# Packed attention and a gated feed-forward layer on one core: batch 1's transposes, v1's permute and v2's load in another order

## The chip, the cores and the metric

One core of a Trainium2 chip runs the whole program. Its engines work at the same time, each through its own queue in order: TensorE (PE, matmuls and transposes; PEld is its weight load), VectorE (DVE), ScalarE (ACT), GpSimd (POOL) and SyncE (SP, which only issues transfers). The metric is the device time of one execution in microseconds (us); lower is better.

## The reference, cut to what matters

For 8 batches of 8 heads, 576 positions and a head dimension of 64, 32 packed queries `p` first attend to keys and values, and then every query attends to the 32 packed results. The output of all heads goes through a feed-forward layer with the activation h cos(h).

```python
def sm_attn(qq, kk, vv):
    s = scale * np.matmul(qq, kk.transpose(0, 1, 3, 2))
    a = np.exp(s - np.max(s, axis=-1, keepdims=True))
    a = a / (np.sum(a, axis=-1, keepdims=True) + 1e-09)
    return np.matmul(a, vv)
p_packed = sm_attn(p, k, v)
out = sm_attn(q, p_packed, p_packed)
x = out.transpose(0, 2, 1, 3).reshape(4608, 512)
h = x @ w_in                      # 512 x 2048
return (h * np.cos(h)) @ w_out    # 2048 x 512
```

## The kernel before

The kernel works batch by batch, with an order written out by hand: what the Python code says first is queued first on each engine.

**One batch.** k, q and v come in as 96 partitions x 8 heads x 384 elements, cast to bf16 by a transfer that POOL issues (`load`, L83). k and q are needed transposed: by PE through PSUM in three groups of eight transposes (`pe_T`, L94 to L106; the matmuls are L103, the copies out of PSUM L74 on ACT or L76 on DVE), or by a transposing transfer on SP (`xbar`, L92). Batches 0 and 1 take `pe_T`, the later ones `xbar`. `permute_v` (L85) copies v into an order by position, on POOL or DVE. `pack_p` (L111) transposes the packed queries of some batches (matmul L116) and copies them into `P2` (DVE, L118); it needs `p_bf`, which POOL casts from `p_raw` (`dup_p`, L327). `s1` computes the packed scores (L128) and their exponentials `a1` (ACT, L137). `a1_pe` transposes `a1` in two halves (L161, copies to `a1T` on DVE), and later batches do it by a transfer (`a1_xbar`, L151). `pp` multiplies `a1T` with the permuted v (L169) and puts the packed result into `ppT` (L175, L179). `s2` makes the second scores (L128 again) and exponentials `a2u` (L210), `sums2` and `normalise` the weights `a2n` (L218 to L228). `ppw` multiplies the packed result with `w_in` in four column blocks (L193, into `PPW`). Then 16 steps `h_mm` follow, one for each block of 128 hidden units: four matmuls (L241), the cosine on ACT (L245), the product on DVE (L248, into `gT`). After steps 7 and 15 POOL copies a rest into `joint` (L252).

**The filler.** The product with `w_out` of a batch is spread over the work of the next one. `out_gen` (L286) yields after each matmul (L294), and `fill(n)` issues n of them. For batch 0 there are 64, and the first 32 take two chunks of output rows in turn, four hidden blocks at a time:

```python
    for f0 in range(0, NFC, 4):
        for c in grp:
            for fc in range(f0, f0 + 4):
```

Hidden block fc reads row block fc of `w_out_bf`, which comes in four loads of four blocks each (`load_w_out`, L322). Steps 12 to 15 of batch 0 issue two fillers each.

**Queues and buffers.** POOL issues all loads in this order: k0, v0, q0, `w_in` in four parts, the rest of p, k1, `w_out` parts 0 and 1, v1, q1, `w_out` parts 2 and 3, k2; then, once v1 has been permuted and batch 0's rests copied, q2, k3, and behind a one-element copy called `gate` (L433), which waits for the transposed k3, v2 and q3. q and v have one input buffer each, k has two. SP issues the transposing transfers and the stores of the output (L301), in order. PSUM has three two-bank buffers `psA` and two one-bank buffers `ot`; the latter hold the filler's sums, and in batch 0's steps the results of `ppw`, `pack_p` and `pe_T` for k1. Four `osb` buffers take the output before it is stored.

**Between the steps of batch 0 and those of batch 1** the order is: s1(1), 4 fillers, q1 transposed, the loads of q2 and k3, 2 fillers, half of a1, 2 fillers, the other half, 3 fillers, pp(1), 5 fillers, s2(1), the first block of ppw(1), the transposes of k2, q2 and k3 on SP, the gate and the loads behind it, 4 fillers, the second block of ppw(1), the weights, 11 fillers, and then `slot(1, ...)` with batch 1's 16 steps.

Of the kernel before, what the change touches and what calls it, by code (L numbers as in the profile page):

```python
# [9 lines left out]
BF16 = mybir.dt.bfloat16  # L10
# [5 lines left out]
def kernel(  # L16
# [37 lines left out]
    V, ACT, G = nc.vector, nc.scalar, nc.gpsimd  # L54
# [17 lines left out]
    def copy(eng, out, in_):  # L72
        if eng is ACT:
            ACT.copy(out=out, in_=in_)  # L74
        else:
            eng.tensor_copy(out=out, in_=in_)  # L76

    def psa(dt=FP32):
        return A.tile([128, 2, 512 if dt == FP32 else 1024], dt, name="psA", tag="A")

    def load(n, b):
        bf[n, b] = bf_pool.tile([TP, H, C * D], BF16, name=n + "bf", tag=n + "bf", bufs=2 if n == "k" else 1)
        G.dma_start(out=bf[n, b], in_=srcs[n][b].rearrange("h (p c) d -> p h (c d)", c=C))  # L83

    def permute_v(b, eng=G):  # L85
        vp[b] = vp_pool.tile([TP, C, H * D], BF16, name="vp", tag="vp")
        copy(eng, vp[b].rearrange("p c (h d) -> p c h d", h=H),
             bf["v", b].rearrange("p h (c d) -> p c h d", c=C))
# [5 lines left out]
    def pe_T(n, b, engs=(V, V, V), groups=(0, 1, 2), own=False):  # L94
        if 0 in groups:
            xT[n, b] = att_pool.tile([128, H * 3, TP], BF16, name=n + "T", tag=n + "T", bufs=2 if n == "k" else 1)
        t = xT[n, b]
        flat = bf[n, b].rearrange("p h x -> p (h x)")
        for i in groups:
            ps = bank(BF16) if own else psa(BF16)[:, 0, :]  # L100
            for j in range(8):
                o = 8 * i + j
                nc.tensor.transpose(ps[:, j * TP:(j + 1) * TP], flat[:, o * 128:(o + 1) * 128],  # L103
                                    ident[0:TP, 0:TP])
            copy(engs[i], t[:, 8 * i:8 * i + 8].rearrange("p a x -> p (a x)"),
                 ps[:, 0:8 * TP])  # L106

    def bank(dt=FP32):
        return O.tile([128, 512 if dt == FP32 else 1024], dt, name="ot", tag="ot")

    def pack_p(b0, b1, flat=None):  # L111
        ng = 2 * (b1 - b0)
        if flat is None:
            flat = psa(BF16).rearrange("p a x -> p (a x)")
        for g in range(ng):
            nc.tensor.transpose(flat[:, g * 128:(g + 1) * 128],  # L116
                                p_bf[:, 2 * b0 + g].rearrange("p t d -> p (t d)"), ident)
        V.tensor_copy(out=P2[:, b0:b1].rearrange("p b h n -> p (b h n)"), in_=flat[:, 0:ng * 128])  # L118
# [14 lines left out]
    def s1(b):  # L133
        ps = scores(P2[:, b], xT["k", b])
        sm = small.tile([128, 2], FP32, name="sums1")
        for y in range(2):
            ACT.activation(  # L137
                out=a1[b % 2][:, y, :, 0:TP].rearrange("p (e m) x -> p e m x", e=2),
                in_=ps[y][:, :, 0:HS].rearrange("p e (m x) -> p e m x", m=3),
                func=AF.Exp, scale=scale, accum_out=sm[:, y:y + 1])  # L140
        sums1[b] = sm
# [12 lines left out]
    def a1_pe(b, ys=(0, 1)):  # L154
        if 0 in ys:
            a1T[b] = att_pool.tile([128, 2, C, 128], BF16, name="a1T", tag="a1T")
        t = a1T[b]
        for y in ys:
            ps = psa(BF16)
            for c in range(C):  # L160
                nc.tensor.transpose(ps[0:TP, 0, c * 128:(c + 1) * 128], a1[b % 2][:, y, c, 0:TP], ident)  # L161
            copy(V, t[0:TP, y].rearrange("p c x -> p (c x)"), ps[0:TP, 0, 0:C * 128])

    def pp(b):
        ps = psa()
        for hp in range(4):
            for j in range(C):
                c = 2 * (j % 3) + j // 3
                nc.tensor.matmul(ps[:, 0, hp * 64:(hp + 1) * 64], vp[b][:, c, hp * 128:(hp + 1) * 128],  # L169
                                 a1T[b][0:TP, :, j, 32 * hp:32 * hp + 32], start=(j == 0), stop=(j == C - 1))  # L170
        pv = ps[:, 0, 0:256].rearrange("p (a y x) -> p a y x", a=4, y=2)
        t = ppT[b % 2].rearrange("p (a y) x -> p a y x", y=2)
        for y in range(2):
            r = slice(64 * y, 64 * y + 64)
            V.tensor_copy(out=t[r, :, y, :], in_=pv[r, :, y, :])  # L175
        for y in range(2):
            r = slice(64 * y, 64 * y + 64)
            z = slice(64 - 64 * y, 128 - 64 * y)
            ACT.copy(out=t[z, :, y, :], in_=pv[r, :, y, :])  # L179

    def ppw(b, n, eng=None, own=False, later=False):
        if b not in PPW:
            PPW[b] = ppw_pool.tile([128, 2, DF], BF16, name="PPW", tag="PPW")
        two = isinstance(eng, tuple)
        if own:
            ps = [bank(), bank()]
        else:
            t = psa()
            ps = [t[:, 0, :], t[:, 1, :]]
        for x in range(4):  # L190
            for y in range(2):
                r = slice(64 * y, 64 * y + 64)
                nc.tensor.matmul(ps[y][32 * x:32 * x + 32, :], ppT[b % 2][r, 2 * x + y, :],  # L193
                                 w_in_bf[r, x, n * 512:(n + 1) * 512], start=True, stop=True)

        def evacuate():
            if own or two:
                for y in range(2):
                    copy(eng[y] if two else eng, PPW[b][:, y, n * 512:(n + 1) * 512], ps[y])
            else:  # L200
                copy(eng or (V, ACT)[n % 2], PPW[b][:, :, n * 512:(n + 1) * 512], t)
        if later:
            return evacuate
        evacuate()

    def s2(b):
        a2u[b] = att_pool.tile([128, 2, S], BF16, name="a2u", tag="a2u")
        ps = scores(ppT[b % 2], xT["q", b])
        for y in range(2):
            ACT.activation(out=a2u[b][:, y].rearrange("p (e x) -> p e x", e=2),  # L210
                           in_=ps[y][:, :, 0:HS], func=AF.Exp, scale=rs1[b][:, y:y + 1])
# [21 lines left out]
    def h_mm(b, fc):  # L233
        if fc == 0:
            gT[b] = g_pool.tile([128, NFC, S], BF16, name="gT", tag="gT")
            if b % 2 == 0:
                joint[b // 2] = j_pool.tile([128, NFC, 128], BF16, name="joint", tag="joint")
        ps = psa()
        for y in range(2):
            for e in range(2):  # L240
                nc.tensor.matmul(ps[:, e, 0:HS], PPW[b][:, y, fc * 128:(fc + 1) * 128],  # L241
                                 a2n[b][:, y, e * HS:(e + 1) * HS], start=(y == 0), stop=(y == 1))
        cs = cos_pool.tile([128, S], BF16, name="cosT")
        csv = cs.rearrange("p (e x) -> p e x", e=2)
        ACT.activation(out=csv, in_=ps[:, :, 0:HS], func=AF.Sin, bias=PI_HALF)  # L245

        def rest():
            V.tensor_tensor(out=gT[b][:, fc, :].rearrange("p (e x) -> p e x", e=2),  # L248
                            in0=ps[:, :, 0:HS], in1=csv, op=ALU.mult)
            if fc % 8 == 7:  # L250
                j0 = (b % 2) * 64
                G.tensor_copy(out=joint[b // 2][:, fc - 7:fc + 1, j0:j0 + 64],  # L252
                              in_=gT[b][:, fc - 7:fc + 1, 512:576])
        return rest
# [56 lines left out]
    def fill(n):  # L311
        while n > 0 and filler[1] > 0:
            next(filler[0])
            filler[1] -= 1
            n -= 1
# [53 lines left out]
    load_w_out(3)  # L369
    dup_p(2, 16, G)  # L370
    load("k", 2)
    permute_v(1, G)
    s2(0)
    ppw(0, 0)
    sums2(0, 0)
# [6 lines left out]
    for fc in range(NFC):  # L382
        h_mm(0, fc)()
        if fc in (3, 6):
            ppw(0, 2 + fc // 6, (ACT, V), own=True)
        if fc == 7:
            pack_p(1, 3, bank(BF16))
        if fc in (9, 10, 11):
            pe_T("k", 1, (V, ACT, V), (fc - 9,), own=True)
        if fc >= 12:  # L390
            fill(2)

# [20 lines left out]

    ACT.preload_act_table_set(EXP_SET)
    s1(1)
    fill(4)
    pe_T("q", 1)
    load("q", 2)
    load("k", 3)
    fill(2)  # L420
    a1_pe(1, (0,))
    fill(2)
    a1_pe(1, (1,))
    recips(1)
    fill(3)
    pp(1)
    fill(5)
    s2(1)
    ppw(1, 0, V)
    xbar("k", 2)  # L430
    xbar("q", 2)
    xbar("k", 3)
    G.tensor_copy(out=gate, in_=xT["k", 3][0:1, 0, 0:1])  # L433
    load("v", 2)
    load("q", 3)
    fill(4)
    ppw(1, 1, V)
# [103 lines left out]
```

## Time and profile before

| | us |
|---|---|
| median of 5 runs | 258.52 |
| the five runs | 258.33, 258.33, 258.52, 259.96, 260.72 |
| the profiled execution, its time | 259.96 |
| its span, first to last instruction | 258.2 |
| PE busy in the span | 239.7 (93%) |
| DVE / ACT / POOL busy | 163.3 / 166.4 / 58.8 |
| 512 matmuls of w_out (L294) | 135.5 |
| 512 matmuls of h (L241) | 83.3 |
| mean granted clock of TensorE | 0.987 |
| moved by DMA | 37.67 MB, 146 GB/s |

The span lies 1.8 us under the time of the same execution. A busy PE is not PE at its peak: matmuls are pipelined, and their ends are modelled, so shares of PE add up to more than the work.

PE is by far the busiest engine over the span, but the share is an average. The front, where the inputs and all weights have to come in, differs from the rest: from 4 to 52 us the DMA engines are busy throughout, at about 205 GB/s.

In the rows below, a line of a timeline gives start, duration, engine, source line, operation, what is written and read, the number of instructions merged, and in brackets how long the engine stood idle before and what ended that.

### The profile page before, as it was taken

The page shows a single profiled execution, that of the slowest core. Times are in us where ns is not written, and L with a number is a line of the kernel's source. Part 1 is how long each engine was busy: PE and PEld are TensorE (multiplying, and loading weights), DVE is VectorE, ACT ScalarE, POOL GpSimd, SP SyncE. Part 2 cuts the span into 40 slices and gives each one's busy share as a digit, 9 for nine tenths or more (in the row PEclk, how much of TensorE's full clock was granted, in tenths as well). Part 3 has the DMA queues.
Part 4 walks back from the last instruction along what each step waited for, and adds up shares of the span by engine and source line. Part 5 has one row for each costly group of instructions (what it writes and reads, how often), then busy time and mean ns, then how long its engine had stood idle before and what let it go on. Part 6 is the DMA issues. An engine that isn't in the chain of part 4 may idle for free.

```text
span 258.2 us, 5022 instructions
## 1 busy us (share of the span) xinstructions
PE 239.7 (93%) x2013; PEld 133.1 (52%) x2013; DVE 163.3 (63%) x252; ACT 166.4 (64%) x272; POOL 58.8 (23%) x70
## 2 busy tenths in 40 slices
PE   8777687989999999999999999999999999999993
PEld 3444445546544555455545654565446554565453
DVE  2549873579837777577856775579656764786110
ACT  1368681397769767886887757777786675874000
POOL 8523316000372222504050405020410000000000
PEclk9999996899999999999999999999999999999999
DMA  6999999998989969999989993989291111111232
GB/s 90 203 207 225 205 204 206 203 175 184 158 139 187 217 137 179 224 206 163 221 117 221 154 203 93 166 172 185 69 188 43 41 43 41 41 43 56 66 81 81
DMA packets 65254, 37.67 MB, mean 146 GB/s; under 512 B 37856, under 2 KB 60640, under 8 KB 65232
## 3 DMA queue, kind: packets, MB, share of 16 engines
q0 software_dynamic: 23168, 18.81, 47.8%
q1 hardware_dynamic: 41904, 18.42, 34.3%
q8 instruction: 15, 0.25, 0.4%
q10 hardware_dynamic: 160, 0.13, 0.2%
q14 instruction: 7, 0.06, 0.1%
HBM read 37.22 MB, written 9.44 MB: 181 GB/s over the span
## 4 chain that ended last, share of the span: by engine, by line
PE 70%; DMA 13%; ACT 8%; DVE 4%; issue 2%; POOL 1%; DVEq 0%; ACTq 0%; POOLq 0%
PE ot L294 41%; PE psA L241 18%; DMA qbf<-in_q_dram 12%; DVE gT L248 3%; PE psA L193 3%; ACT cosT L245 2%; ACT a2u L210 2%; DMA a1T<-a 2%; PE psA L169 1%; PE psA L218 1%; PE psA L128 1%; PE ot L280 1%; PE psA L103 1%; ACT L481 1%; PE psA L161 1%
## 5 line engine op out<-in xcount | busy, mean ns | idle before, releaser
L294 PE MATMUL ot<-w_out_bf,gT 128*128 128x512 bf16 x512 | 135.5, 383 | 0.0
L248 DVE TENSOR_TENSOR gT<-psA,cosT 128x576 bf16<-128x576 f32 x128 | 93.0, 754 | 30.0 <-ACT cosT L245 28.7
L245 ACT ACTIVATE cosT<-psA 128x576 bf16<-128x576 f32 x128 | 81.8, 652 | 26.7 <-PE psA L241 25.0
L241 PE MATMUL psA<-a2n,PPW 128*128 128x288 bf16 x512 | 83.3, 286 | 3.2 <-DVE gT L248 1.9
L294 PEld LDWEIGHTS <-gT 128*128 128x128 bf16 x512 | 48.0, 98 | 42.4 <-issue 6.5
L241 PEld LDWEIGHTS <-PPW 128*128 128x128 bf16 x512 | 49.7, 98 | 36.8 <-issue 7.5
L76 DVE CAST PPW<-psA 128x1024 bf16<-128x1024 f32 (+1 forms) x24 | 27.0, 1132 | 11.4 <-PE psA L193 11.4
L252 POOL COPY joint<-gT 128x512 bf16<-128x512 bf16 x16 | 9.8, 616 | 79.0 <-DVE gT L248 79.0
L76 POOL COPY vp<-vbf 96x3072 bf16<-96x3072 bf16 x7 | 19.7, 2809 | 17.9 <-DMA vbf<-in_v_dram 17.9
L76 DVE COPY osb<-ot 128x512 f32<-128x512 f32 (+1 forms) x19 | 12.8, 672 | 16.9 <-PE ot L294 13.8
L74 ACT COPY osb<-ot 128x512 f32<-128x512 f32 (+1 forms) x18 | 10.3, 573 | 18.5 <-PE ot L294 13.8
L228 DVE SCALAR_TENSOR_TENSOR a2n<-a2u,r,lns 128x576 bf16<-128x576 bf16 x16 | 12.4, 815 | 11.5 <-ACT lns L226 11.5
L179 ACT CAST ppT<-psA 64x128 bf16<-64x128 f32 x16 | 4.2, 260 | 19.2 <-DVE ppT L175 16.2
L220 ACT ACTIVATE lns<-psA 128x576 f32<-128x576 f32 x16 | 10.3, 652 | 5.8 <-PE psA L218 5.3
L137 ACT ACTIVATE a<-psA 128x576 bf16<-128x576 f32 x16 | 10.3, 649 | 4.2 <-PE psA L128 4.1
L294 PE MATMUL ot<-w_out_bf,joint 128*128 128x512 bf16 x48 | 12.8, 379 | 0.0
L210 ACT ACTIVATE a2u<-psA,rs 128x576 bf16<-128x576 f32 x16 | 11.0, 737 | 1.3 <-PE psA L128 1.0
L193 PE MATMUL psA<-w_in_bf,ppT 64*32 64x512 bf16 x232 | 10.8, 381 | 0.9 <-DVE gT L248 0.5
L245 ACT ACT_TABLE_LOAD x8 | 10.3, 1283 | 0.1
L226 ACT ACTIVATE lns<-lns 128x576 f32<-128x576 f32 x16 | 10.0, 678 | 0.0
L332 PE MATMUL ot<-wz 128*128 128x512 bf16 x25 | 8.4, 489 | 1.2 <-DVE wz L344 1.2
L74 ACT CAST PPW<-psA 128x1024 bf16<-128x1024 f32 (+1 forms) x9 | 7.3, 821 | 3.2 <-PE psA L193 3.2
(65 smaller groups left out, 144.8 us busy)
## 6 DMA issues: line engine op xcount, KB each, us to landing
kbf<-in_k_dram POOLq DMA_DIRECT2D x8, 576.0 KB, 11.8
vbf<-in_v_dram POOLq DMA_DIRECT2D x8, 576.0 KB, 6.5
qbf<-in_q_dram POOLq DMA_DIRECT2D x8, 576.0 KB, 8.8
out_dram<-osb SPq DMA_DIRECT2D x24, 192.0 KB, 2.4
out_dram<-osb SPq DMA_DIRECT2D x22, 128.0 KB, 2.4
w_in_bf<-in_moe_w_in_dram POOLq DMA_DIRECT2D x4, 512.0 KB, 14.9
w_out_bf<-in_moe_w_out_dram POOLq DMA_DIRECT2D x4, 512.0 KB, 20.9
out_dram<-osb SPq DMA_DIRECT2D x26, 64.0 KB, 2.0
```

The source lines that it names most:

```text
L74: ACT.copy(out=out, in_=in_)
L76: eng.tensor_copy(out=out, in_=in_)
L137: ACT.activation(out=a1[b % 2][:, y, :, 0:TP].rearrange("p (e m) x -> p e m x", e=2), in_=ps[y][:, :, 0:HS].rearrange("p e (m x) -> p e m ...
L193: nc.tensor.matmul(ps[y][32 * x:32 * x + 32, :], ppT[b % 2][r, 2 * x + y, :], w_in_bf[r, x, n * 512:(n + 1) * 512], start=True, stop=True)
L210: ACT.activation(out=a2u[b][:, y].rearrange("p (e x) -> p e x", e=2), in_=ps[y][:, :, 0:HS], func=AF.Exp, scale=rs1[b][:, y:y + 1])
L220: ACT.activation(out=lns[b][:, y].rearrange("p (e x) -> p e x", e=2), in_=ps[:, :, 0:HS], func=AF.Ln)
L226: ACT.activation(out=lns[b][:, y], in_=lns[b][:, y], func=AF.Exp, scale=-1.0)
L228: V.scalar_tensor_tensor(out=a2n[b][:, y], in0=a2u[b][:, y], scalar=r1[b][:, y:y + 1], in1=lns[b][:, y], op0=ALU.mult, op1=ALU.mult)
L241: nc.tensor.matmul(ps[:, e, 0:HS], PPW[b][:, y, fc * 128:(fc + 1) * 128], a2n[b][:, y, e * HS:(e + 1) * HS], start=(y == 0), stop=(y == 1))
L245: ACT.activation(out=csv, in_=ps[:, :, 0:HS], func=AF.Sin, bias=PI_HALF)
L248: V.tensor_tensor(out=gT[b][:, fc, :].rearrange("p (e x) -> p e x", e=2), in0=ps[:, :, 0:HS], in1=csv, op=ALU.mult)
L294: nc.tensor.matmul(pss[c], w, w_out_bf[:, fc, :], start=(fc == 0), stop=(fc == NFC - 1))
```

## The change

The packed-key transposes of batches 1 and 2 go from step 7 of batch 0 to step 12, behind k1's transposes. v1 is permuted by DVE right after s1(1), not by POOL. q1 is transposed behind pp(1), no longer behind the first four fillers, and with it go the loads of q2 and k3 that stand behind it. The numbers of fillers between are 8, 2, 3 and 4 where they were 4, 2, 2, 3 and 5. v2's load stands directly behind k3's, no longer behind the gate. The order of POOL's loads among each other stays as it was.

```diff
--- before.py
+++ after.py
@@ -369,7 +369,6 @@
     load_w_out(3)
     dup_p(2, 16, G)
     load("k", 2)
-    permute_v(1, G)
     s2(0)
     ppw(0, 0)
     sums2(0, 0)
@@ -383,10 +382,10 @@
         h_mm(0, fc)()
         if fc in (3, 6):
             ppw(0, 2 + fc // 6, (ACT, V), own=True)
-        if fc == 7:
-            pack_p(1, 3, bank(BF16))
         if fc in (9, 10, 11):
             pe_T("k", 1, (V, ACT, V), (fc - 9,), own=True)
+        if fc == 12:
+            pack_p(1, 3, bank(BF16))
         if fc >= 12:
             fill(2)
 
@@ -413,25 +412,25 @@
 
     ACT.preload_act_table_set(EXP_SET)
     s1(1)
-    fill(4)
-    pe_T("q", 1)
-    load("q", 2)
-    load("k", 3)
-    fill(2)
+    permute_v(1, V)
+    fill(8)
     a1_pe(1, (0,))
     fill(2)
     a1_pe(1, (1,))
     recips(1)
     fill(3)
     pp(1)
-    fill(5)
+    pe_T("q", 1)
+    load("q", 2)
+    load("k", 3)
+    load("v", 2)
+    fill(4)
     s2(1)
     ppw(1, 0, V)
     xbar("k", 2)
     xbar("q", 2)
     xbar("k", 3)
     G.tensor_copy(out=gate, in_=xT["k", 3][0:1, 0, 0:1])
-    load("v", 2)
     load("q", 3)
     fill(4)
     ppw(1, 1, V)
```

## The prediction

> **What bounds the kernel now.** I read the page's slices first, then the chain of waits from 36 to 56 us, then PE's timeline and a table of windows over the same stretch, and last the landing of single DMA issues.
>
> ```profile
> PEclk9999996899999999999999999999999999999999
> DMA  6999999998989969999989993989291111111232
> ```
>
> Of 40 slices of 6.45 us the granted clock falls in two alone, from 38.7 to 51.6 us, while the DMA engines are full. From slice 8 on PE is busy nine tenths and the chain is nearly all PE: a microsecond lost at the front stays lost. The change lies in and around these two slices. The chain there:
>
> ```profile
> 19.65 20.72 DMA qbf<-in_q_dram
> 40.37 0.05 issue
> 40.41 1.46 PE psA L103 x16
> ...
> 47.75 1.08 PE ot L294 x5
> 48.83 0.57 PE psA L128 x16
> ```
>
> q1's load, issued at 19.65, lands at 40.37; all that follows hangs on it, up to the second scores (s2(1), L128) at 48.8. PE's timeline:
>
> ```profile
> 36.48 0.56 PE L128 MATMUL psA<-kT,P 64*32 64x288 bf16 x16
> 36.98 1.04 PE L294 MATMUL ot<-w_out_bf,gT 128*128 128x512 bf16 x4
> 40.41 2.27 PE L103 MATMUL psA<-ident,qbf 96*128 96x96 bf16 x24 [2.40 <-DMA qbf<-in_q_dram]
> 42.48 1.05 PE L294 MATMUL ot<-w_out_bf,gT 128*128 128x512 bf16 x2
> ```
>
> After s1(1) and four filler matmuls PE stands 2.40 us for q1. Then everything takes twice its time: two fillers 1.05 us, where four took 1.04. The windows (PE, PEld, DVE, ACT, POOL busy; clock; DMA share; GB/s) give the same:
>
> ```profile
> 38.02:40.41 2.39, 0.00 (x0) 0.00 (x0) 0.00 (x0) 1.46 (x5) 2.39 (x2) 0.96 1.26 207
> 40.41:47.04 6.63, 6.62 (x49) 4.63 (x50) 3.02 (x7) 0.00 (x0) 2.54 (x4) 0.50 1.27 203
> 47.04:48.76 1.72, 1.72 (x29) 0.94 (x26) 0.58 (x2) 0.26 (x1) 0.00 (x0) 1.00 1.31 204
> ```
>
> The stall costs 2.4 us and half of 6.63 at clock 0.50, 3.3 more: 5.7 us in all. Transfers move 203 to 207 GB/s here, so landing times are set by the order of issue on the POOL queue. The load of third w_out rows, issued at 21.91:
>
> ```profile
> w_out_bf<-in_moe_w_out_dram POOLq DMA_DIRECT2D x1, 512.0 KB, 21.0
> ```
>
> It lands at 42.9. The fourth, issued 24.59 and 20.9 us under way, lands at 45.5; v1 at 37.5 (16.60 + 20.9); k1 at 29.4 (8.36 + 21.1); k2 at 48.4 (28.71 + 19.7). The change moves no load that stands ahead of these in the queue, so I take all of these times over.
>
> **Packed-key transposes behind k1's.** Before, PE waits 1.89 us in step 7 (until 28.82) for POOL's p_bf. After, steps 8 and 9 (1.14 us as at 29.05) follow at 26.93 and end near 28.1, and the next wait is k1's landing: 1.3 us instead. From the first k1 transposes (30.03) to s1(1) (36.48) went 6.45 us; the four moved transposes add 0.23 (28.82 to 29.05), and a wait of 0.48 for VectorE's copy of kT may go. So s1(1) at 29.45 + 6.45 + 0.23 = 36.1, or 35.7. VectorE copies P2 0.42 us as before. Gain 0.3 to 0.8, but only up to the next fixed landing.
>
> **v1 on VectorE.** POOL loses 2.75 us, for which only its two joint copies waited. VectorE gets 0.96 (batch 0's row at 10.57), after v1 lands at 37.5. Queued behind it are the a1T copies, whose transposes cannot start before ScalarE's first exponential: it ran 38.12 to 38.77. VectorE idles 3.67 us here now. Cost nothing; if v1 came 1 us later, it would delay those copies, and pp(1), by about that.
>
> **q1 behind pp(1).** Eight fillers in a row, 8 x 0.26 = 2.1 (from four in 1.04), run from 36.6 to 38.1 or a bit more, then a1_pe's first half (0.54) until about 38.5. Then fill(2). Fillers are yielded one matmul at a time: eight in steps 12 to 15 and these eight use up w_out rows 0 to 7 of both chunks. The 17th reads row block 8, of the third load: PE stands until 42.95. In the kernel before, the 17th came at 45.5 and found it landed. So the wait is not removed but changes its owner: 42.95 instead of 40.41, 4.4 us instead of 2.40, with less work left behind it.
>
> That work, at half clock by the chain's rows from 40.41 to 48.76: two fillers 0.85, six a transposes 0.64, three fillers 1.28, pp 1.2 (estimate: 24 took 0.80 in a stretch of which most had full clock), 24 q transposes 2.07, four fillers 1.7: 7.7 us, s2(1) at 50.7. At full clock: 0.43 + 0.54 + 0.65 + 0.80 + 1.2 + 0.87 = 4.5, and about 0.5 because the third q group needs the PSUM buffer of pp, which VectorE and ScalarE empty in 0.61 + 0.55: 47.9. How much of it has half clock? 2.40 us of idling cost 6.8 us of it before; 4.4 us I take to cost as much, but its start is open: from 40.2 on as before, it would hold until 47.0 and s2(1) comes near 49.2; from 43.6, until 50.4. I take 50.0, the upper middle, because the slow time seen before began when the stall was nearly over: 1.2 later than 48.76. Bounds: -0.9 and +2.0.
>
> A rule speaks against this edit. The Trainium skill, "TensorE: Matmul & The Clock Gate", section "Why this matters for your kernels", asks for no idle gaps over about 3 us, since the clock then halves; its window (3.4 us) is said to run freely. Here 2.40 us was enough, so the measurement goes below the rule. By the rule alone only the new gap would halve the clock, by the row both do; the sum would be the same.
>
> 17 fillers instead of 16 stand ahead of s2(1): one less later, -0.22 (217 ns each at full clock).
>
> **q2, k3 and v2 loads.** On POOL q2 waits for the last q1 transpose. That was 42.68, and becomes about 48.5, so the queue runs dry after k2 (48.4). A load alone takes 6.4 us (v2 at 65.32); q2 lands near 55 (51.25 before), k3 near 58 (54.75), v2 near 61. On SP the transposes of q2 and k3 wait for these; k3's landed 10.0 us after its load (64.76), so 68 now. Needed: kT3 by s1(3) at 75.2, qT2 by s2(2) at 77.7, each about a microsecond later now. Seven us of cover; beyond it each us is a PE stall. SP's stores queue behind k3's transposes: four o buffers hold all of batch 0's chunks, and the next is filled after 70. v2 ahead of the gate: its permute is no longer tied to a landing at 71.75, but to the gate (68), q3's issue (0.77) and a joint copy (0.62): done near 72.3 instead of 74.55, while pp(2) stood at 75.58 and shows no wait for it. Worth 0 here. v3 and k4 go 2 us earlier; from this, or from PE's own delay, pp(4)'s wait of 0.59 us for a1T can vanish: 0 to -0.6, taken -0.3.
>
> **Sum.** The profiled execution took 259.96 us (span 258.2): + 1.2 - 0.2 - 0.3 gives 260.7, 0.8% over the median of 258.52. Three of the five runs lie at 258.33 to 258.52; whether they, too, had the half clock, no row tells. With the stall but full clock s2(1) would stand 3.3 earlier; pp(2) would then wait about 2.3 for v2 (its cover is 1.0), so 1.0 would be left: 259.0. That is near those runs, a sign that the half clock does not fall on each of them.
>
> **Rivals.**
> - *The replaced wait costs little* (0.24): the same theft by w_out, but with half clock seldom or short, or the shift of +0.7 applied to 258.5. For it: the tight group of runs and s2(1) at 47.9 (259.96 - 0.9 - 0.2 - 0.3 = 258.6). 258.5 to 259.9.
> - *The slow clock outlasts the stage* (0.15), clearly slower: half clock until about 54, as the long gap spans two periods. fill(11) then takes 5.4 us for 2.54, of which the chain from s2(1) to the first h matmul (48.76 to 53.98, nearly all PE) hides next to nothing: s2(1) at 50.7 (+2.0) and another 0.3 to 2.0. It decides once the clock is still 0.5 at 51 us. 261.6 to 263.5.
> - *The stall really goes* (0.06), the other side: if third w_out rows land before they are wanted, 5.7 us vanish up to s2(1), v2 is early enough not to take it back, and 254 to 255.5 results. Against: the landing at 42.9, behind q1 in the same queue.
> - That v2's early load slows the gate by its own transfer (about 3 us, the spacing of loads in the full queue) is inside the seven us above.
>
> **Numbers.** My forecast (259.9 to 261.6, likeliest 260.7) has 0.55. From no change a measurement can tell about 1%: 255.9 to 261.1. About two thirds of the forecast lies below 261.1 (0.36), with the first rival 0.60 for within 1%; slower 0.19 + 0.15 = 0.34; faster 0.06. The range 258.5 to 262.2 leaves out the last rival, and the outer parts of the other two.
>
> **What would show it.** PE waiting in L294 for w_out_bf until 42.9, right after the first six L161 transposes, with no wait of L103 for q; k1's transposes waiting for kbf until 29.4 and L116 for nothing; the granted clock at 0.5 somewhere between 41 and 51; s2(1) near 50; q2's issue near 48.5; pp(2) and pp(4) without waits. I am wrong if the 17th filler does not wait, if the clock stays full, or if PE stands for kT or qT near 70 to 78.

## The result and the profile after

| | before | after |
|---|---|---|
| median (runs) | 259.19 us (48) | 260.67 us (27) |
| lowest and highest | 257.54, 263.8 | 259.01, 264.33 |
| profiled execution: time, span | 259.96, 258.2 | 259.26, 257.1 |
| its mean granted clock | 0.987 | 0.999 |

The ratio is 1.0054, with a 95% interval from 1.0033 to 1.0076: about 1.4 us slower, under the 1% that a measurement of this kernel was taken to tell. The median of before moved from the 258.52 of five runs to 259.19 with 48.

The two profiles shown do not compare like with like: the changed kernel's has the shorter span, although its median is the longer. Its profiled execution is also one of its fastest (259.26, with 259.01 the lowest), and that of the kernel before one of the slower half. The slices of the page after (first the granted clock, then the DMA engines) show what else differs:

```profile
PEclk9999999999999999999999999999999999999999
DMA  6999999699999979999989994989291111112232
```

Counted from 0, slices 6 and 7 had the lower clock before; in this execution they have full clock. In the DMA row slice 7 (45 to 51 us) falls from 9 to 6: from 45.35 on only k2 is left of the loads, until q2 is issued at 47.39. The chain of waits after, over the same stretch (start, duration, what):

```profile
22.02 20.78 DMA w_out_bf<-in_moe_w_out_dram
42.80 0.04 issue
42.84 0.59 PE ot L294 x2
...
47.95 0.37 PE psA L128 x16
```

Where q1's load stood there now stands the third part of w_out, landing at 42.80. PE's timeline after (start, duration, line, operation, count, and in brackets the idle time before it and what ended it):

```profile
37.13 0.56 PE L128 MATMUL psA<-kT,P 64*32 64x288 bf16 x16
37.63 1.90 PE L294 MATMUL ot<-w_out_bf,gT 128*128 128x512 bf16 x8
39.56 0.54 PE L161 MATMUL psA<-ident,a 128*96 128x128 bf16 x6
42.84 0.59 PE L294 MATMUL ot<-w_out_bf,gT 128*128 128x512 bf16 x2 [2.74 <-DMA w_out_bf<-in_moe_w_out_dram]
...
47.88 0.44 PE L128 MATMUL psA<-qT,ppT 64*32 64x288 bf16 x16
```

The wait for q1 before L103 is gone. After eight fillers and six transposes the next filler stands 2.74 us. From there PE works at full clock, and s2(1) starts at 47.88, 5.1 us behind the landing; before, it was 8.4 us behind q1's. Two windows of the profile after (PE, PEld, DVE, ACT, POOL busy; clock; DMA share; GB/s):

```profile
40.10:42.84 2.74, 0.00 (x1) 0.00 (x0) 0.55 (x1) 0.04 (x1) 0.00 (x0) 1.00 1.25 207
42.84:47.88 5.04, 4.40 (x63) 2.90 (x62) 2.95 (x8) 0.52 (x2) 0.49 (x1) 1.00 0.89 140
```

A fair comparison needs the kernel before with full clock at this place, or the changed kernel with the half clock; the experiments gave both.

### The profile page after: what moved, and what is told of

Its sections match the earlier page's. It is cut to its first block, busy times and chain, and to the rows that moved or that the text cites. A ratio compares the mean times of both kernels' runs of the same rounds, so it can differ in the third digit from the quotient of the medians.

```text
span 257.1 us, 5020 instructions
## 1 busy us (share of the span) xinstructions
PE 236.4 (92%) x2013; PEld 130.8 (51%) x2013; DVE 164.6 (64%) x253; ACT 166.6 (65%) x272; POOL 56.4 (22%) x69
## 4 chain that ended last, share of the span: by engine, by line
PE 65%; DMA 14%; ACT 8%; DVE 7%; issue 2%; POOL 2%; DVEq 0%; ACTq 0%; POOLq 0%
PE ot L294 40%; PE psA L241 17%; DMA w_out_bf<-in_moe_w_out_dram 8%; DMA w_in_bf<-in_moe_w_in_dram 6%; DVE gT L248 6%; ACT cosT L245 3%; PE psA L193 3%; PE ot L280 1%; PE psA L218 1%; PE psA L169 1%; PE psA L128 1%; ACT a2u L210 1%; ACT L480 1%; DVE osb L76 1%; ACT osb L74 1%
## 5 line engine op out<-in xcount | busy, mean ns | idle before, releaser
L294 PE MATMUL ot<-w_out_bf,gT 128*128 128x512 bf16 x512 | 133.7, 379 | 3.3 <-DMA w_out_bf<-in_moe_w_out_dram 2.7
L294 PEld LDWEIGHTS <-gT 128*128 128x128 bf16 x512 | 47.9, 98 | 46.2 <-issue 9.9
L252 POOL COPY joint<-gT 128x512 bf16<-128x512 bf16 x16 | 10.5, 657 | 87.2 <-DVE gT L248 87.2
L74 ACT COPY osb<-ot 128x512 f32<-128x512 f32 (+1 forms) x18 | 10.3, 573 | 18.5 <-PE ot L294 13.8
L76 POOL COPY vp<-vbf 96x3072 bf16<-96x3072 bf16 x6 | 16.5, 2751 | 6.9 <-DMA vbf<-in_v_dram 6.9
L332 PE MATMUL ot<-wz 128*128 128x512 bf16 x25 | 7.5, 450 | 1.2 <-DVE wz L344 1.2
```

What stands on the lines that cost most here:

```text
L294: nc.tensor.matmul(pss[c], w, w_out_bf[:, fc, :], start=(fc == 0), stop=(fc == NFC - 1))
```

## The experiments

All ratios are to the kernel before on the same chip.

**The kernel before, again.** No edit.

> The kernel before once more, to see its granted clock run by run beside its time. Clock theory (the runs' spread is the half clock falling on some of them): runs at a clock near 1.00 lie together, those near 0.987 (6.8 us of half clock) 1.5 to 3.3 us above them. Rival (the half clock is absorbed later, the spread has another source): time does not follow the clock. Both: ratio 1.00.

Measured: ratio 0.9997 (0.996 to 1.0035), median 259.49; mean clock per run between 0.983 and 0.993, time from 257.56 to 262.84. No run had a clock above 0.993, so the clock theory's comparison could not be made as it was put. The profiled execution is the fastest of the twelve (span 255.8 us) at the lowest mean clock, 0.983: the mean clock over the whole execution does not order the times, and to that extent the rival holds. PE's timeline of this execution shows that the place of the half clock differs:

```profile
28.73 0.61 PE L116 MATMUL ot<-ident,p_bf 128*128 128x128 bf16 x4 [1.46 <-POOL p_bf L327]
...
39.97 0.85 PE L103 MATMUL psA<-ident,qbf 96*128 96x96 bf16 x16 [0.87 <-DMA qbf<-in_q_dram]
...
45.68 0.64 PE L128 MATMUL psA<-qT,ppT 64*32 64x288 bf16 x16
...
73.27 0.87 PE L169 MATMUL psA<-a1T,vp 96*128 96x64 bf16 x24 [0.71 <-DVE rs L147]
```

The half clock fell earlier (15.1 to 18.5 and 28.7 to 32.2 us); PE comes to q1 later and waits only 0.87 us, and q1's stretch has full clock. So s2(1) is at 45.68, 3.1 us ahead of the first profile. Further on pp(2) stands 0.71 us: the row names DVE, but POOL's permute of v2 ends at 73.21, just before it:

```profile
70.47 2.74 POOL L76 COPY vp<-vbf 96x3072 bf16<-96x3072 bf16 x1 [5.10 <-DMA vbf<-in_v_dram]
```

Set beside the changed kernel at full clock:

| us | s2(1) | s1(2) | pp(2) | s2(2) | span |
|---|---|---|---|---|---|
| before, again | 45.68 | 67.23 | 73.27 | 75.37 | 255.8 |
| after | 47.88 | 69.30 | 74.57 | 76.67 | 257.1 |
| difference | 2.20 | 2.07 | 1.30 | 1.30 | 1.3 |

These are two single executions, but their spans differ by about as much as the medians (1.5 us). The change costs 2.2 us up to s2(1); 0.8 of that come back at pp(2), where the kernel before waits for v2; 1.3 us reach the end, which is 0.5%, as measured. Not all of the 2.2 is the wait: about 0.35 us is that the loads landed earlier in the one execution (q1 at 39.92 against 40.27), and 0.22 that the changed kernel has one filler more ahead of s2(1).

**Matmuls in the gaps.** Their results are not used; the rest of the computation is whole.

```diff
 (before)                      (after)
     fill(4)                       a1_pe(1, (0,))
+    warm_a(10)               +    warm_a(11)
     pe_T("q", 1)                  fill(2)
```

> The kernel before, with ten idle-time matmuls of 512 columns (about 2.2 us) in the 2.40 us in which PE waits for q1; their result is not used. Clock theory: the half clock behind the stall is gone, the mean clock is 0.995 or more in every run, and where the kernel before had it the time falls by 1 to 2 us, so 0.2 to 0.6% in the median. Rival (the stall itself is the cost, the clock is not): ratio 1.00, within 0.2%.

> The changed kernel, with eleven idle-time matmuls (about 2.4 us) behind the first half of the a transposes, in the 2.74 us in which PE waits for the third part of w_out; their result is not used. Clock theory: the changed kernel's median of 260.7 against its profiled 259.3 is half clock behind the longer gap; with the gap filled the runs gather at 259.0 to 259.8, and the ratio to the kernel before is 0.997 to 1.003. Rival (the wait for w_out is the whole loss): no better than the changed kernel, 1.004 to 1.007.

Measured: before_dense 0.9977 (0.9945 to 1.0009), after_dense 1.0018 (0.9984 to 1.0053). For the changed kernel the clock theory's range is met: 9 of 12 runs at a clock of 0.995 or more, median 258.66. For the kernel before the expectation failed in one half: only 1 of 12 runs reached 0.995, as its half clock falls in other places too (29.1 to 32.5 in the profile, behind the wait for p_bf, here 2.0 us). Both intervals touch those of the unfilled kernels, so how much the clock is worth is not measured sharply. Filled against filled, 1.0018 / 0.9977 = 1.004, but these intervals overlap too, and the medians (258.66 and 258.17) lie only 0.2% apart. The two profiles say more. Both have full clock from 33 to 60 us. First before_dense, then after_dense (L337 is the filling):

```profile
38.79 2.32 PE L337 MATMUL psA<-wz 128*128 128x512 bf16 x10
...
46.19 0.64 PE L128 MATMUL psA<-qT,ppT 64*32 64x288 bf16 x16
```

```profile
43.06 0.59 PE L294 MATMUL ot<-w_out_bf,gT 128*128 128x512 bf16 x2 [0.34 <-DMA w_out_bf<-in_moe_w_out_dram]
...
48.10 0.44 PE L128 MATMUL psA<-qT,ppT 64*32 64x288 bf16 x16
```

With both gaps filled and full clock behind them, s2(1) is still 1.9 us later in the changed kernel, and so is the end of the span (257.9 against 256.0). In these executions it is the wait, not the clock. (The filling of before_dense runs until 41.1, past q1's landing at 39.87, so it delays q1's transposes by about a microsecond: it is not simply the kernel before at full clock.)

**The third part of w_out ahead of q1.**

```diff
+    load_w_out(2)
     load("q", 1)
-    load_w_out(2)
     load_w_out(3)
```

> The changed kernel, with the third part of w_out loaded ahead of q1 and not behind it. Wait theory: the 17th filler no longer waits (its rows land near 40.3), q1 lands near 42.8 and is wanted near 42.0, so PE waits 0.8 us for it; the 25th filler then waits for the fourth part until 45.4, and the second scores start near 45.7, 2.2 us ahead of the 47.9 in the changed kernel; 1 to 2.5 us faster than it, a ratio of 0.996 to 1.001 to the kernel before. Rival (what the change loses, it loses in the moved packed-key transposes or in the later loads): the ratio stays at 1.004 to 1.007 although the wait is gone.

Measured: 0.9964 (0.9932 to 0.9996), median 258.16, in the same set as before_again. PE's timeline:

```profile
42.39 1.36 PE L103 MATMUL psA<-ident,qbf 96*128 96x96 bf16 x24 [0.46 <-DMA qbf<-in_q_dram]
43.80 0.59 PE L294 MATMUL ot<-w_out_bf,gT 128*128 128x512 bf16 x2
44.93 0.38 PE L294 MATMUL ot<-w_out_bf,gT 128*128 128x512 bf16 x1 [0.54 <-DMA w_out_bf<-in_moe_w_out_dram]
45.23 0.44 PE L128 MATMUL psA<-qT,ppT 64*32 64x288 bf16 x16
```

The long gap has become two short ones, and s2(1) stands at 45.23, half a microsecond ahead of the 45.7 expected, as the fourth part landed at 44.88 and not at 45.4. Exchanging two loads turns 0.5% slower into about 0.4% faster: the landing that the moved fillers read was the loss. The clock does not explain it: after_dense, in the same set, has the wait filled with matmuls and the same 9 of 12 runs at a clock of 0.995 or more, and stands at 1.0018 (the two intervals overlap by a little).

**The changed kernel again, and v2 back behind the gate.**

```diff
     load("k", 3)
-    load("v", 2)
 ...
     G.tensor_copy(out=gate, in_=xT["k", 3][0:1, 0, 0:1])
+    load("v", 2)
     load("q", 3)
```

> The changed kernel once more, as the common base of this set. Wait theory: PE waits 2.5 to 3 us for the third part of w_out, s2(1) starts near 47.9 where the clock is full, ratio 1.003 to 1.008. Rival (nothing but drift between chips): 1.000 within 0.2%.

> The changed kernel, with v2's load back behind the gate. Theory (the early v2 gives back part of what the w_out wait takes): s2(1) unchanged near 47.9; k3's transposes land near 67, v2 is issued near 67.5, lands near 74, is permuted near 77, and pp(2), due at 74.6, waits about 2 us for it; 1.5 to 2.5 us slower than the changed kernel, ratio 1.010 to 1.015. Rival (v2's early transfer costs more by contention than it brings): as fast as the changed kernel or faster, 1.000 to 1.005.

Measured: after_again 1.0052 (1.0007 to 1.0097), with a 2.86 us wait and s2(1) at 47.87. after_v2gate 1.0103 (1.0039 to 1.0166). POOL's and PE's timelines of after_v2gate:

```profile
67.45 0.77 POOL L83 DMA_DIRECT2D vbf<-in_v_dram  x1 [0.36 <-DVE gT L248]
...
74.87 2.74 POOL L76 COPY vp<-vbf 96x3072 bf16<-96x3072 bf16 x1 [5.27 <-DMA vbf<-in_v_dram]
```

```profile
77.67 0.87 PE L169 MATMUL psA<-a1T,vp 96*128 96x64 bf16 x24 [1.41 <-DVE rs L147]
```

The permute ends at 77.61 and pp(2) starts at 77.67, after 1.41 us of waiting (2 were expected; PE came later, as this execution had half clock from 43.3 to 46.7 and s2(1) at 49.52). So v2's early load is the useful part of the change; without it the changed kernel is about 1% slower than the kernel before, not 0.5%. The intervals of the two runs overlap, none of the six runs of after_v2gate has a clock of 0.995 or more, and the verdict rests on the wait, which only one of them has.

**q1 transposed in the gap, and v2 permuted ahead of the gate.** The first of the two edits:

```diff
     fill(8)
-    a1_pe(1, (0,))
-    fill(2)
-    a1_pe(1, (1,))
+    a1_pe(1)
     recips(1)
-    fill(3)
-    pp(1)
-    pe_T("q", 1)
+    pe_T("q", 1, (V, ACT, V))
     load("q", 2)
     load("k", 3)
     load("v", 2)
-    fill(4)
+    pp(1)
+    fill(5)
     s2(1)
```

The second adds `permute_v(2)` in front of the gate and takes it out of step 8 of batch 1.

> The changed kernel, with both halves of a1 and then q1 transposed right behind the eight fillers (q1's middle copy on ScalarE), and pp(1) and five fillers behind them, so that the first filler that reads the third part of w_out stands at about 42.8. Wait theory: no wait of PE over 1 us between 37 and 46, s2(1) near 44, 3.9 us ahead of the changed kernel and 1.7 ahead of the kernel before; v2 is permuted near 70 and pp(2) starts near 71; ratio 0.989 to 0.995. Rival (the order there does not matter, since later transfers set pp(2) and pp(4)): s2(1) earlier, but the ratio not below 0.997.

> The same, with v2 permuted by POOL ahead of the gate and not in step 8 of batch 1. Theory (pp(2) hangs on v2's permute once PE is early): v2 is permuted before 66, pp(2) starts when PE comes to it, near 70.8, and the time falls by another 0 to 0.6 us, ratio 0.988 to 0.994. Rival (pp(2) no longer hangs on v2): equal to the run without this step within 0.2%.

Measured: q_in_gap 0.9903 (0.9867 to 0.994), median 256.37, lowest 255.68; faster than both kernels. PE's timeline:

```profile
38.99 1.17 PE L161 MATMUL psA<-ident,a 128*96 128x128 bf16 x12
39.99 1.31 PE L103 MATMUL psA<-ident,qbf 96*128 96x96 bf16 x24
41.53 0.86 PE L169 MATMUL psA<-a1T,vp 96*128 96x64 bf16 x24 [0.23 <-DVE qT L76]
42.23 1.25 PE L294 MATMUL ot<-w_out_bf,gT 128*128 128x512 bf16 x5
43.41 0.64 PE L128 MATMUL psA<-qT,ppT 64*32 64x288 bf16 x16
```

q1, landed at 39.60, is transposed in the time in which the changed kernel stood still, and the filler that needs the third part comes when it is there. No wait over 0.23 us shows in this stretch, 10 of 12 runs have a clock of 0.995 or more, and s2(1) is at 43.41. That is 4.5 us ahead of the changed kernel's profile, but the span is only 3.2 us shorter. Two things flatter s2(1): only 13 fillers stand ahead of it, where the changed kernel has 17, and the third part landed at 42.14 in this execution, where it was 42.80. And later a filler waits for ScalarE to empty an output buffer, which neither the expectation nor the profiles of the two kernels had:

```profile
48.82 1.02 PE L294 MATMUL ot<-w_out_bf,gT 128*128 128x512 bf16 x4 [1.14 <-ACT osb L74]
```

q_gap_v2first, where the third part landed at 42.79, has s2(1) at 44.25. Its ratio is 0.9893 (0.9837 to 0.995), and pp(2) stands without a wait in both runs (71.13 and 71.98): not to be told apart. The rival held for this step: with PE this early, v2 was permuted at 69.9 and in time anyway.

**Packed-key transposes back in step 7**, in the changed kernel and in q_in_gap.

```diff
+        if fc == 7:
+            pack_p(1, 3, bank(BF16))
         if fc in (9, 10, 11):
             pe_T("k", 1, (V, ACT, V), (fc - 9,), own=True)
-        if fc == 12:
-            pack_p(1, 3, bank(BF16))
```

> The changed kernel, with the packed-key transposes back in step 7. Theory (the moved transposes cost PE 0.6 us up to s1(1), since they and k1's copies share two PSUM buffers, but the fixed landing of w_out's third part swallows it): s1(1) near 36.5 where the changed kernel had 37.0 to 37.4, the wait in the filler 3 to 3.7 us instead of 2.8, s2(1) again near 47.9, ratio 1.003 to 1.008. Rival (the move is part of the loss): s2(1) earlier by 0.5 us or more, ratio 1.000 to 1.003.

> The kernel with q1 transposed in the gap, with the packed-key transposes back in step 7. Theory: q1's landing (39.6 to 40.3) is the next thing that PE meets, so of the 0.6 us at s1(1) 0 to 0.4 reach s2(1), and a short wait for q1 shows; ratio 0.988 to 0.992, not to be told from the run without this step. Rival (the move costs its whole 0.6 us here, where nothing stands for w_out): 0.6 us faster than that run.

Measured: after_pack7 1.0069 (1.0033 to 1.0105), s1(1) at 36.77, a wait of 3.24 us: the gain is swallowed, as the theory said. That s2(1) would again be near 47.9 did not hold in this execution, which shows the changed kernel's gap with the half clock behind it (windows, columns as above):

```profile
39.74:42.98 3.24, 0.00 (x1) 0.00 (x0) 0.55 (x1) 0.04 (x1) 0.00 (x0) 0.78 1.24 206
42.98:48.39 5.41, 5.41 (x51) 4.01 (x51) 1.89 (x6) 0.45 (x2) 0.00 (x0) 0.50 0.79 124
```

Here s2(1) is at 49.80 and the span 259.2, against 48.76 and 258.2 in the first profile of the kernel before, which had it too: 1.0 us in both places.

q_gap_pack7: 0.9937 (0.9896 to 0.9979), median 258.26, not the 0.988 to 0.992 expected. In its profiled execution (wait for p_bf 1.8 us, span 254.5) s1(1) stands at 36.31, 0.25 us ahead of q_in_gap, and nothing of that reaches s2(1) at 43.69: the filler now waits 0.37 us for the third part. That fits the theory, and not the rival's 0.6 us. But its runs fall into two groups, near 256.0 and near 258.4, and only 5 of 12 have a clock of 0.995 or more. q_in_gap differs from it in the moved transposes alone and has 10 of 12. So the move may pay here, and by the clock, but that is not shown: one run of the slower group has a clock of 1.00 and one of the faster 0.993. The two were measured on different chips, their intervals overlap, and the idle gap ahead of k1 does not explain it by its length: it was 1.0 us in q_in_gap's profile, but 1.8 in q_gap_v2first's, whose six runs all kept the clock. Whether and how the move helps the clock stays open.

## Why the prediction was right

The forecast of a slower kernel within 1% held for the reason given: the wait was not removed but passed from q1 to the third part of w_out. The range held the time. That 260.7 was met to the tenth is luck: the terms gave +0.7 us on an execution of 259.96, which lies 0.8 above the median of 48 runs, where the measured change is +1.4 us on that median.

- **Its own signs.** The prediction said it would be wrong if the clock stayed full, and in the profile after it did: s2(1) stands at 47.88 there and not near 50. So this half of the mechanism, that the longer gap costs as much half clock as the old one, holds for some executions only (after_v2gate with 3.4 us of half clock, after_pack7 with 6.8) and not for the two profiles of the changed kernel itself. The other signs came: the 17th filler waits, L103 does not wait for q1 and L116 not for p_bf, and PE waits for neither kT nor qT from 50 to 120 us.
- **Fixed landings.** q1 at 40.27, w_out at 42.80, k2 at 48.31 after: all within 0.12 us of what the profile before gave. Over all profiles with this order of loads the third part landed between 42.14 and 43.02. That the POOL queue's order sets them is what everything else rests on; after_swap shows it, where the exchanged loads land in the exchanged order (w_out at 39.45, q1 at 42.34).
- **Packed-key transposes.** I had 0.3 to 0.8 us gained up to s1(1); it came 0.65 later, at 37.13. The wait for k1 was 1.69 us, then the third group of k1 waited 0.59 us for ScalarE's copy and the first filler 0.59 for VectorE's: by the program these neighbours share the two `ot` buffers of PSUM. The prediction counted the old wait of 0.48 at most, and not a second one. Putting the transposes back gave 0.2 to 0.5 us at s1(1). The fixed landing swallowed the loss, as the prediction said of the gain.
- **v1 on VectorE.** It ran from 38.17 for 0.95 us, and VectorE then stood idle for 1.03 us until the first a transposes: no cost, as forecast. No run undoes this step alone.
- **The new wait.** 4.4 us forecast, 2.74 measured. The step that was mis-sized is the end of a1_pe's first half, put at 38.5; it ended at 40.1. One microsecond of that is s1(1) at 37.13 instead of 36.1. The rest lies in the sum: eight fillers of 0.26 us from 36.6 on end at 38.7, not at the 38.1 written there (they took 1.90 us and ended at 39.53), and the transposes took 0.54. They started at 39.56, right behind both the fillers and ScalarE's first exponential (39.42, its sum 39.51). The landing, and so s2(1), is not moved by that.
- **s2(1).** 47.9 without and up to 50.7 with the half clock were forecast, 50.0 taken. The runs show 47.88 and 47.87 (after, after_again), and 49.52 and 49.80 (after_v2gate, after_pack7): both cases exist.
- **The sum.** "+1.2 - 0.2 - 0.3" was made on a profile with the half clock. With it in both, the measured sum is +1.0 (259.2 in after_pack7, against 258.2); without it, +2.2 at s2(1) and -0.9 up to the end. Near the same 1 us, from other terms.
- **v2.** "Worth 0 here" was right for the profile at hand, and wrong where the kernel before has full clock at q1: there it gives back 0.8 us. When it is undone, 1.4 us of wait appear, even in an execution with half clock. The paragraph on the sum had this wait in its second case, but as 2.3 us, with v2's load left where it was; in before_again that load was issued at 63.23 and not at 65.32, and the wait is 0.71.
- **Later loads.** q2, k3 and v2 landed at 53.4, 57.7 and 61.8 (55, 58, 61 forecast), k3's transposes at 68.7 (68), v2's permute ended at 73.3 (72.3), and PE waited for none of them. pp(4)'s wait for a1T shrank from 0.59 to 0.36, by 0.2 us where 0.3 was taken.

On the clock, the Trainium skill ("TensorE: Matmul & The Clock Gate", section "Why this matters for your kernels") asks for no idle gaps over about 3 us. Here gaps of 1.46 us (before_again), 2.0 (before_dense) and 2.40 (before) already had half clock behind them, so the measurements go below the figure. Gaps of 2.74 (after) and 2.86 us (after_again) had none, which agrees with it, but one of 2.79 (after_v2gate) had: length alone does not decide.

## What to carry to other kernels

When a step that waits for a transfer is put later, list every transfer that the steps pulled ahead of it read, with its landing time; the next one behind it in a full queue takes over the wait. Move work that has all its operands into the gap, rather than work that is merely not the one that waits. And before comparing two profiles look at the granted clock in the stretch itself: one execution's half clock here hid, in the two profiles first compared, a difference of 1.3 us.

## What was not expected of the hardware

Every stretch between two changes of the clock inside the profiled spans was a multiple of 3.41 us (34.1, 6.8, 10.2, 3.4, 23.9, 37.5), at another offset in every execution, as if the clock were decided anew in fixed slots that do not know the program. Two windows of such slots, first of the profile after (the clock held), then of after_pack7 (it halved at the end of the slot):

```profile
38.35:41.77 3.42, 1.72 (x12) 0.75 (x11) 1.32 (x2) 1.78 (x5) 1.24 (x1) 1.00 1.25 206
41.77:45.18 3.41, 2.34 (x37) 1.61 (x37) 0.80 (x3) 0.00 (x0) 0.00 (x0) 1.00 1.28 205
```

```profile
38.14:41.55 3.41, 1.56 (x11) 0.71 (x10) 1.16 (x2) 1.63 (x5) 1.08 (x1) 1.00 1.25 205
```

A gap of 2.74 us that is split between two slots left 1.72 and 2.34 us busy and cost nothing more; one of 3.24 us left 1.56 in the first of its slots and the clock was halved for 6.8 us; one of 2.79 that lay in a single slot (39.86 to 43.28 in after_v2gate) left 0.63 and the clock was halved for 3.4 us. But PE's busy time in a slot does not decide it alone. A slot with 1.52 us busy (26.56 to 29.97 in the first profile of the kernel before) did not halve the clock; one with 1.67 (25.33 to 28.74 in its repetition) did, and so did one with 2.21 and no gap over 0.73 us, ahead of the other stretch of half clock in that repetition:

```profile
11.68:15.09 3.41, 2.21 (x50) 1.84 (x47) 2.14 (x7) 0.95 (x3) 0.88 (x2) 1.00 1.26 205
15.09:18.50 3.41, 3.10 (x31) 1.32 (x30) 1.78 (x2) 2.48 (x5) 0.79 (x1) 0.50 1.24 207
```

What else decides it stays open. The same kernel can so run with its half clock in one place or in another, and the changed one also with none up to its end. That may be part of the spread from 257.5 to 264 us. It is not all of it: runs at a clock of 1.00 spread from 259.2 to 261.8 after, and in after_swap those at 0.995 or more lie in two groups, near 256.4 and near 258.4.
